# Five raw weight buffers for four, four low-word buffers for five, and one gather moved into the middle of an expert's second layer

## The chip, the cores and the metric

The kernel runs on one core of one Trainium2 chip. The metric is the device time of one execution in microseconds (us). The engines go by short names: PE is TensorE (PEld its weight loads), ACT ScalarE, DVE VectorE, POOL GpSimd, SP SyncE, whose queue issues the plain transfers; POOL issues the indirect ones (gathers and scatters of rows).

## The reference, cut to what matters

Three stages follow each other on 1792 rows of 768 numbers, all in float32: an attention with a sigmoid for a softmax, a layer of eight experts in which each expert takes 224 rows, and a wide layer of 2048.

```python
attn = 1.0 / (1.0 + np.exp(-scores))            # 4 x 12 heads of 448 x 448
x = np.matmul(attn, v)                          # 1792 x 768 after a transposition
...
for e in range(E):                              # E = 8, cap = 224 rows each
    mask = assigned == e
    h = np.maximum(x[mask] @ w1[e], 0.0)        # 768 -> 1024
    out[mask] = h @ w2[e]                       # 1024 -> 768
...
r = np.maximum(x @ w_in, 0.0)                   # 768 -> 2048
return (s * (r * r) + b) @ w_out                # 2048 -> 768
```

Which rows go to which expert is settled by a bidding of all rows for all experts.

## The kernel before, in words

**Two words for one number.** PE multiplies in a format that keeps fewer bits than float32. So each operand is split into a high word (the number in that format) and a low word (what is left), and each product is taken as high by high, high by low and low by high. For a weight tile this is a chain of three steps: SP asks for the raw tile of 128 x 768 float32 (384 KB) into the pool `wraw`; ACT casts it to the high word `wh` (line 242, `w_high`, pool `wsp` with five buffers); DVE, for some tiles POOL, subtracts to get the low word `wl` (line 252, `w_low`, pool `wlp`). The raw buffer is free again when the low word is done; the low-word buffer is free again when PE's last product with it is done.

**One list of tiles.** All weight tiles of the expert layer and of the wide layer stand in one list, `units`, in the order in which PE uses them. Counters say how far each step of the chain has come: `dma`, `pre`, `high`, `low`, and `use` for PE. After each step of PE's work `advance()` (line 752) moves them on: requests up to 8 tiles past `use`, low words up to `use + ahead - 1`, high words up to `use + ahead`, with `ahead` 5 (3 or 4 in the mixed layer). What an engine has in its queue is run in order, so a low word that stands behind a slow instruction waits with it.

**An expert** (`expert`, line 774; they are counted from 0 here, as in the code). Its first layer has eight steps, one weight tile each: six by `half_mm`, in which one matmul of 448 columns takes high and low word of the input side by side, and two by `short_mm`. Its second layer has six steps of eight pairs of matmuls; its eight tiles hold six column blocks each, so a step eats one tile and a third. After the matmuls of a step, ACT copies half of the sum out of PSUM (line 718), DVE adds the other half (719), `advance()` follows, and then `done` splits the result into high and low word for the next layer (lines 725 and 726, or 780 and 781).

**Rows of the experts.** `gather(e)` (line 603) has POOL fetch an expert's 224 rows by index in two parts of 128 and 96 rows, 3 KB each, into the two buffers of the pool `xrp`. `x_split(e, n)` turns a quarter of them on PE (704) and splits them on ACT and DVE (706, 707); for experts 6 and 7 this stands in the first layer of the expert before. So a gather must come after the last `x_split` of the expert before it and before the first of its own. For experts 6 and 7 it is issued between the two layers of experts 4 and 5. During the first layer of expert 4 POOL also issues six scatters of result rows (line 853).

**After the experts.** Experts 0 and 1, and 2 and 3, are followed by `layer_in` (the wide layer's first half for 448 rows); after 3 comes `outputs` (the second half), which writes 896 rows. After expert 7 come `layer_mixed` and `outputs` once more; there some tiles are sums and differences of others, formed on DVE in `w_pre`.

Of the kernel before, what the change touches and what calls it, by code (L numbers as in the profile page):

```python
# [28 lines left out]
KD = DM // 128  # L29
KF = F1 // 128  # L30
# [33 lines left out]
def tile_kernel(ctx, tc, qT, kT, v, wg, w1, w2, wi, wo, s2, b2, cst, out):  # L64
# [1 line left out]
    V, A, G, T = nc.vector, nc.scalar, nc.gpsimd, nc.tensor  # L66

    const = ctx.enter_context(tc.tile_pool(name="const", bufs=1))
    wraw = ctx.enter_context(tc.tile_pool(name="wraw", bufs=4))
    wsp = ctx.enter_context(tc.tile_pool(name="wsp", bufs=5))  # L70
    wlp = ctx.enter_context(tc.tile_pool(name="wlp", bufs=5))
    xrp = ctx.enter_context(tc.tile_pool(name="xrp", bufs=2))
    dpool = ctx.enter_context(tc.tile_pool(name="dpool", bufs=1, space=DRAM))
    ctx.enter_context(tc.manual_schedule())
# [103 lines left out]
    raws, splits, sums = {}, {}, {}  # L178
    nu = {"dma": 0, "pre": 0, "high": 0, "low": 0, "use": 0, "ahead": 5}
# [14 lines left out]
    for g in range(4):  # L194
# [3 lines left out]
        more = [narrow[f] for f in range(KG)] if g < 2 else []  # L198
        if g == 3:
            more = [(0, 1), (1, 1), (0, 2), (1, 2), (0, 3), (1, 3), (0, 4)]  # L200
# [45 lines left out]
    def w_low(eng=None):  # L246
        i = nu["low"]
        if i < nu["high"]:
            r, h = w_source(i), splits[i]
            lo = wlp.tile([128, KD, 128], F32R, name="wl")[:, :r.shape[1]]  # L250
            eng = eng or (G if where[i] else V)
            eng.tensor_sub(lo, r, h.bitcast(F32))  # L252
            splits[i] = (h, lo)
            nu["low"] += 1

    def w_get():
        i = nu["use"]
        nu["use"] += 1
        return splits.pop(i)
# [343 lines left out]
    def gather(e):  # L603
        if e >= E:
            return
        for h, n in enumerate(HT):
            if (e, h) not in xr:
                xr[e, h] = xrp.tile([128, DM], F32, name="xr")
            G.indirect_dma_start(out=xr[e, h][:n], out_offset=None, in_=xs,
                                 in_offset=bass.IndirectOffsetOnAxis(ap=idx[:n, h, e:e + 1], axis=0))  # L610
# [69 lines left out]
    def row_ids():  # L680
        def put(dst, rows, h, col, r0, n, src):
            for r in range(0, n, 32):
                G.tensor_copy(dst[rows + r:rows + r + 32, col], idx[r0 + r:r0 + r + 32, h, src])

        a, b = slice(0, E, 2), slice(1, E, 2)
        put(idt[:, 0], 0, 0, slice(0, 4), 64, 64, a)
        put(idt[:, 0], 64, 1, slice(0, 4), 0, 64, a)
        put(idt[:, 1], 0, 1, slice(0, 4), 64, 32, a)
        put(idt[:, 1], 32, 0, slice(0, 4), 0, 96, b)
        put(idt[:, 2], 0, 0, slice(0, 4), 96, 32, b)  # L690
        put(idt[:, 2], 32, 1, slice(0, 4), 0, 96, b)
        put(idl, 0, 0, slice(0, 2), 0, 64, slice(0, 4, 2))
        put(idl, 64, 0, slice(0, 2), 0, 64, slice(4, E, 2))
# [15 lines left out]
    def half_mm(weights, src, n, done, ahead, tt=None):  # L709
        p = ps_m.tile([128, 512], F32, name="acc")  # L710
        for k in range(n):
            wh, wl = weights(k)
            T.matmul(p[:, :2 * CAP], wh, src[:, k].rearrange("p a s -> p (a s)"), start=(k == 0), stop=False)  # L713
            T.matmul(p[:, :CAP], wl, src[:, k, 0], start=False, stop=(k == n - 1))  # L714
        t2 = pool["y"].tile([128, 2, CAP], F32, name="tmp", bufs=pool["tmp"])
        bs = t2[:, 0]
        tt = t2[:, 1] if tt is None else tt
        A.copy(bs, p[:, CAP:2 * CAP])  # L718
        V.tensor_add(tt, p[:, :CAP], bs)
        if ahead:  # L720
            advance()
        done(tt, bs)

    def two(dst, src):
# [13 lines left out]
    def w_dmas():  # L738
        while nu["dma"] < min(nu["use"] + 8, len(units)):
            w_dma()  # L740

    def w_lows():
        while nu["low"] < min(nu["use"] + nu["ahead"] - 1, nu["high"]):
            w_low()

    def w_highs():
        while nu["high"] < min(nu["use"] + nu["ahead"], len(units)):
            if nu["pre"] == nu["high"]:
                w_pre()
            w_high()  # L750

    def advance():
        w_dmas()
        w_lows()
        while nu["pre"] < min(nu["use"] + nu["ahead"] + 1, nu["dma"]):
            w_pre()
        w_highs()
# [16 lines left out]
    def expert(e, y):  # L774
        x = xg.pop(e)
        u = ml.tile([128, KF, 2, CAP], F32R, name="u")

        def first(f):
            def done(tt, _):
                A.activation(u[:, f, 0], tt, AF.Relu)  # L780
                V.scalar_tensor_tensor(u[:, f, 1], tt, 0.0, u[:, f, 0].bitcast(F32), op0=ALU.max, op1=ALU.subtract)  # L781

            return done

        for f in range(KF):
            wh, wl = w_get()
            if f < KF - 2:
                half_mm(lambda k: (wh[:, k], wl[:, k]), x, KD, first(f), f < KF - 3)
                if f == KF - 3:
                    advance()  # L790
            else:
                short_mm(wh, wl, x, KD, (u[:, f, 0], u[:, f, 1]))
                if f == KF - 2:
                    advance()
            if 1 <= f <= 4 and (e % 2 == 0 or e == 5):
                x_split(e + 1, f - 1)
            if f >= 1 and out_rows:
                scatter(*out_rows.pop(0))
        if e in (4, 5):
            gather(e + 2)  # L800
        sl = slice((e % 2) * CAP, (e % 2 + 1) * CAP)
        held = []
        if e == 6:
            mov["b22"] = m2p.tile([128, HK, 2, S], F32R, name="x")
        elif e == 7:
            mov["t3"] = m2p.tile([128, HK, 2, S], F32R, name="x")

        def halves(name, d, cols=sl):
            return mov[name][:, d, 0, cols], mov[name][:, d, 1, cols]

        for d in range(KD):
            def second(k):
                n, c = divmod(d * KF + k, KD)
                if n == len(held):
                    held.append(w_get())
                return [w[:, c] for w in held[n]]

            def done(tt, spare):
                if e < 6:
                    two((y[:, d, 0, sl], y[:, d, 1, sl]), tt)  # L820
                    return
                if d < HK:
                    V.tensor_sub(spare, tt, full(0, d, sl))
                    work = [(halves("t1", d), spare)]
                    if e == 7:
                        work.append((halves("t3", d, slice(0, CAP)), full(1, d, slice(0, CAP))))
                else:
                    V.tensor_sub(full(1, d - HK, sl), full(1, d - HK, sl), tt)
                    work = [(halves("b22", d - HK), tt)]
                    if e == 7:  # L830
                        work.append((halves("t3", d - HK), full(1, d - HK, sl)))
                for dst, src in work:
                    A.copy(dst[0], src)
                for dst, src in pending:
                    V.tensor_sub(dst[1], src, dst[0].bitcast(F32))
                pending[:] = work
                if e == 7 and d in (0, 1):
                    mix(2 - d, slice(0, CAP))

            tt = None  # L840
            if e in (4, 5):
                tt = full(d // HK * 2, d % HK, sl)
            elif e > 5 and d < HK:
                tt = full(1, d, sl)
            half_mm(second, u, KF, done, d < KD - 1, tt)
            if not e and d == 1:
                row_ids()
            if e == 1 and 2 <= d <= 4:
                late_do(f"a{d - 2}", 0)

    def scatter(ids, row):
        G.memset(spacer, 0.0)
        st = G.indirect_dma_start(out=out, out_offset=bass.IndirectOffsetOnAxis(ap=ids, axis=0), in_=row,
                                  in_offset=None)
        for o in stores:
            tc.declare_no_dep(st.ins, o.ins, reason="different rows")
        stores.append(st)
# [104 lines left out]
    def ahead(st, n, more=()):  # L962
        def lows():
            while na["low"] < min(n + 3, na["high"]):
                a_low(st)

        def sums():
            while na["sum"] < min(n + 5, 28):
                a_sum(st)

        w_dmas()
        work, more = [w_lows, lows, sums], list(more)
        while work or more:
            for q in (work, more):
                if q:
                    q.pop(0)()
        w_highs()
        while na["high"] < min(n + 4, 28):
            a_high(st)
# [261 lines left out]
```

## Time and profile before

| what | value |
|---|---|
| median of 3 runs | 916.81 us (915.82 to 917.8) |
| the profiled execution | 918.23 us, span 916.4 us |
| busy: PE, PEld | 879.4 us (96%), 755.4 us (82%) |
| busy: DVE, ACT, POOL | 659.4 us (72%), 519.5 us (57%), 130.0 us (14%) |
| mean transfer rate | 187 GB/s |

The span is the time from the first to the last instruction; the execution's own time has a little around it. A share of busy time is a mean over the whole kernel and says nothing of which engine holds up which in one stage. In a row of the timeline, the bracket at its end is the time that the engine was idle before the instruction, with what ended it. A raw tile is `raw`, its high word `wh`, its low word `wl`; `xr` are gathered rows, `px` and `acc` are tiles in PSUM.

### The profile page before, as it was taken

To read this page: it belongs to the slowest core of one execution; us is meant where nothing else is said; L and a number is where in the kernel's file an instruction comes from. 1 tells how busy PE (TensorE), PEld (TensorE's weight loads), DVE (VectorE), ACT (ScalarE), POOL (GpSimd) and SP (SyncE) were. 2 spreads that over 40 slices of the span, in tenths; PEclk is the share of its full clock that TensorE was granted. 3 is DMA by queue.
4 is the path that set the end of the run, shared out by engine and by line. 5 is a ranking of instruction groups with operands and counts; after the bars stand their busy time and mean duration, and the time that the engine had idled before them with its cause. 6 is when DMAs were issued, how large, how long until landed. Compare 5 with 4: busy or idle time off the path is not lost.

```text
span 916.4 us, 14216 instructions
## 1 busy us (share of the span) xinstructions
PE 879.4 (96%) x5219; PEld 755.4 (82%) x5219; DVE 659.4 (72%) x1101; ACT 519.5 (57%) x895; POOL 130.0 (14%) x131
## 2 busy tenths in 40 slices
PE   9999999789999999999999999899997999999997
PEld 4554555559989989999999998898996899999997
DVE  3877885646678777689767855877897788768680
ACT  6666666736555565643565545666655455654540
POOL 1000003222600033300000035422300000000003
PEclk9999999769999999999999999999998999999999
DMA  9989994755768775759643438665541212332213
GB/s 291 332 289 350 313 325 163 214 168 164 220 210 287 246 253 177 228 178 324 218 141 123 128 123 278 201 206 174 193 138 52 69 53 69 104 120 94 97 35 138
DMA packets 70186, 171.52 MB, mean 187 GB/s; under 512 B 8160, under 2 KB 25056, under 8 KB 70112
## 3 DMA queue, kind: packets, MB, share of 16 engines
q1 hardware_dynamic: 67840, 159.56, 53.3%
q0 software_dynamic: 2272, 11.01, 3.4%
q8 instruction: 42, 0.69, 0.3%
q14 instruction: 32, 0.26, 0.1%
HBM read 142.23 MB, written 28.31 MB: 186 GB/s over the span
## 4 chain that ended last, share of the span: by engine, by line
PE 52%; DVE 9%; DMA 7%; issue 5%; ACT 3%; POOL 1%; POOLq 0%; ACTq 0%; DVEq 0%; SPq 0%
DMA raw<-in_w_dram 7%; PE acc L1014 6%; PE acc L1016 6%; PE acc L1017 6%; PE acc L860 4%; PE acc L861 4%; PE acc L862 4%; PE acc L713 4%; DVE wl L252 4%; PE acc L1108 3%; PE acc L1106 3%; PE acc L1107 3%; PE acc L714 2%; ACT wh L242 1%; DVE u L781 1%
## 5 line engine op out<-in xcount | busy, mean ns | idle before, releaser
L242 ACT CAST wh<-raw 128x768 fp32r<-128x768 f32 (+1 forms) x240 | 195.5, 823 | 119.5 <-issue 48.0
L252 DVE TENSOR_TENSOR wl<-raw,wh 128x768 fp32r<-128x768 f32 (+1 forms) x199 | 191.9, 971 | 45.4 <-ACT wh L242 45.0
L252 POOL TENSOR_TENSOR wl<-raw,wh 128x768 fp32r<-128x768 f32 x41 | 82.5, 2016 | 439.9 <-ACT wh L242 439.8
L713 PE MATMUL acc<-u,wh 128*128 128x448 f32 x384 | 122.9, 378 | 1.6 <-DVE u L736 1.3
L714 PE MATMUL acc<-u,wl 128*128 128x224 f32 x384 | 102.3, 266 | 2.5 <-DVE wl L252 2.5
L302 ACT ACTIVATE attn<-psc,nls 112x896 f32<-112x896 f32 x96 | 88.8, 1008 | 10.1 <-PE psc L300 10.1
L713 PE MATMUL acc<-x,wh 128*128 128x448 f32 x288 | 93.7, 380 | 0.6 <-issue 0.6
L713 PEld LDWEIGHTS acc<-u,wh 128*128 128x128 f32 x384 | 72.8, 189 | 8.4 <-DVE u L736 3.0
L714 PE MATMUL acc<-x,wl 128*128 128x224 f32 x288 | 76.6, 266 | 2.3 <-DVE wl L252 2.3
L311 PE MATMUL pv<-attn,vt 112*64 112x448 f32 x384 | 77.5, 546 | 0.0
L714 PEld LDWEIGHTS acc<-u,wl 128*128 128x128 f32 x384 | 74.1, 193 | 2.8 <-DVE wl L252 2.8
L860 PE MATMUL acc<-y,wh 128*128 128x448 f32 x192 | 71.2, 371 | 0.9 <-ACT y L725 0.9
L861 PE MATMUL acc<-y,wh 128*128 128x448 f32 x192 | 70.6, 368 | 0.0
L862 PE MATMUL acc<-y,wl 128*128 128x448 f32 x192 | 70.3, 366 | 0.0
L311 PEld LDWEIGHTS pv<-attn,vt 112*64 112x64 f32 x384 | 25.4, 136 | 43.0 <-issue 36.1
L714 PEld LDWEIGHTS acc<-x,wl 128*128 128x128 f32 x288 | 55.0, 191 | 3.4 <-DVE wl L252 3.4
L713 PEld LDWEIGHTS acc<-x,wh 128*128 128x128 f32 x288 | 54.1, 188 | 4.5 <-issue 0.8
L1014 PE MATMUL acc<-wh,as 128*128 128x384 f32 x168 | 56.3, 335 | 0.0
L1017 PE MATMUL acc<-wh,as 128*128 128x384 f32 x168 | 56.2, 334 | 0.0
L1016 PE MATMUL acc<-wl,as 128*128 128x384 f32 x168 | 56.1, 334 | 0.0
L718 ACT COPY tmp<-acc 128x224 f32<-128x224 f32 x96 | 32.6, 340 | 21.1 <-PE acc L714 20.4
L781 DVE SCALAR_TENSOR_TENSOR u<-tmp,u 128x224 fp32r<-128x224 f32 x48 | 30.6, 639 | 18.0 <-ACT u L780 18.0
(341 smaller groups left out, 2027.9 us busy)
## 6 DMA issues: line engine op xcount, KB each, us to landing
raw<-in_w_dram SPq DMA_DIRECT2D x128, 384.0 KB, 3.5
raw<-nw SPq DMA_DIRECT2D x72, 384.0 KB, 3.2
craw<-in_wi_dram SPq DMA_DIRECT2D x16, 768.0 KB, 6.1
raw<-mx SPq DMA_DIRECT2D x32, 384.0 KB, 2.9
nw<-co SPq DMA_DIRECT2D x24, 384.0 KB, 6.9
craw<-in_wo_dram SPq DMA_DIRECT2D x8, 768.0 KB, 5.6
ra<-in_wo_dram SPq DMA_DIRECT2D x8, 768.0 KB, 6.4
rqk<-in_kT_dram SPq DMA_DIRECT2D x24, 224.0 KB, 6.6
```

Source lines behind the costliest of these rows:

```text
L242: A.copy(h, r)
L252: eng.tensor_sub(lo, r, h.bitcast(F32))
L302: A.activation(attn[n][:, :, c, :], p[:, :, :S], AF.Sigmoid, bias=nls[:CP], scale=1.0 / math.sqrt(D))
L311: T.matmul(pv[j * 64:(j + 1) * 64, :S], v[:, c, j * D:(j + 1) * D], a[:, j, c, :], start=(c == 0), stop=(c == NC - 1))
L713: T.matmul(p[:, :2 * CAP], wh, src[:, k].rearrange("p a s -> p (a s)"), start=(k == 0), stop=False)
L714: T.matmul(p[:, :CAP], wl, src[:, k, 0], start=False, stop=(k == n - 1))
L860: T.matmul(p, wh, src[:, k, 0], start=first, stop=False)
L861: T.matmul(p, wh, src[:, k, 1], start=False, stop=False)
L862: T.matmul(p, wl, src[:, k, 0], start=False, stop=last)
L1014: T.matmul(acc, hi, wh[:, cols], start=(opens[j] and u == 0 and c == 0), stop=False, skip_group_check=True)
L1016: T.matmul(acc, hi, wl[:, cols], start=False, stop=False, skip_group_check=True)
L1017: T.matmul(acc, lo, wh[:, cols], start=False, stop=(u == 3 and c == 1), skip_group_check=True)
```

## The change

The raw pool gets a fifth buffer and the low-word pool loses one; the memory is the same. `advance` takes a number: with 1, low words go as far ahead as before; with 2, one tile less far. The second layers of the experts and `outputs` use 2, first layers, `layer_in` and `layer_mixed` use 1. The gather of expert 6's rows moves from the end of expert 4's first layer to the third step of its second layer; that of expert 7's rows stays between the layers of expert 5.

```diff
-    wraw = ctx.enter_context(tc.tile_pool(name="wraw", bufs=4))
+    wraw = ctx.enter_context(tc.tile_pool(name="wraw", bufs=5))
     wsp = ctx.enter_context(tc.tile_pool(name="wsp", bufs=5))
-    wlp = ctx.enter_context(tc.tile_pool(name="wlp", bufs=5))
+    wlp = ctx.enter_context(tc.tile_pool(name="wlp", bufs=4))
...
         if ahead:
-            advance()
+            advance(ahead)
...
-    def w_lows():
-        while nu["low"] < min(nu["use"] + nu["ahead"] - 1, nu["high"]):
+    def w_lows(n=1):
+        while nu["low"] < min(nu["use"] + nu["ahead"] - n, nu["high"]):
             w_low()
...
-    def advance():
+    def advance(n=1):
         w_dmas()
-        w_lows()
+        w_lows(n)
...
-                half_mm(lambda k: (wh[:, k], wl[:, k]), x, KD, first(f), f < KF - 3)
+                half_mm(lambda k: (wh[:, k], wl[:, k]), x, KD, first(f), int(f < KF - 3))
...
-        if e in (4, 5):
-            gather(e + 2)
+        if e == 5:
+            gather(7)
...
-            half_mm(second, u, KF, done, d < KD - 1, tt)
+            half_mm(second, u, KF, done, 2 if d < KD - 1 else 0, tt)
             if not e and d == 1:
                 row_ids()
+            if e == 4 and d == 2:
+                gather(6)
...
-        work, more = [w_lows, lows, sums], list(more)
+        work, more = [lambda: w_lows(2), lows, sums], list(more)
```

The order in which the instructions stand, at three places. First SP's queue where expert 0's second layer begins: the transfer of a wide weight in raw form into `ra`, and then the first requests for raw tiles, with the semaphores that each waits for (DMAHW is a transfer's own, DVE, Pool and Activation the engines'). Before:

```order
L867 DMA ra_2744<-in_wo_dram 128x1536 [waits Activation_sequencer_49,PE_sequencer_49,Pool_sequencer_49,DVE_sequencer_49,DVE_49,SP_sequencer_49,PE_49,DMAHW4_49,Activation_49,Pool_49]
L218 DMA raw_2769<-in_w2_dram 128x768 [waits DMAHW5_49,DVE_49,Activation_49]
L218 DMA raw_2793<-in_w2_dram 128x768 [waits DMAHW6_49,Pool_49]
L218 DMA raw_2826<-in_w2_dram 128x768 [waits DMAHW7_49,DVE_49]
L218 DMA raw_2856<-in_w2_dram 128x768 [waits DMAHW0_49,DVE_49,Activation_49]
```

and now:

```order
L869 DMA ra_2744<-in_wo_dram 128x1536 [waits Activation_sequencer_49,PE_sequencer_49,Pool_sequencer_49,DVE_sequencer_49,DVE_49,SP_sequencer_49,PE_49,DMAHW4_49,Activation_49,Pool_49]
L218 DMA raw_2769<-in_w2_dram 128x768 [waits DMAHW5_49]
L218 DMA raw_2793<-in_w2_dram 128x768 [waits DMAHW6_49,DVE_49,Activation_49]
L218 DMA raw_2826<-in_w2_dram 128x768 [waits DMAHW7_49,DVE_49,Activation_49]
L218 DMA raw_2856<-in_w2_dram 128x768 [waits DMAHW0_49,Pool_49]
```

The requests are the same and stand in the same order, but the waits have moved down by one: the first request waits for no low word any more, and POOL's low word is waited for two requests later.

Second, POOL's queue from expert 4's first layer (the last two scatters into `out_dram`) to the gathers into `xr` for experts 6 and 7. Before:

```order
L853 DMA out_dram<-rb,idt 1792x768
L609 DMA xr<-xs,idx 128x768
L609 DMA xr<-xs,idx 96x768
L252 TENSOR_TENSOR wl<-raw,wh 128x768 x5
L609 DMA xr<-xs,idx 128x768
L609 DMA xr<-xs,idx 96x768
L252 TENSOR_TENSOR wl<-raw,wh 128x768 x11
```

and now:

```order
L855 DMA out_dram<-rb,idt 1792x768
L252 TENSOR_TENSOR wl<-raw,wh 128x768
L609 DMA xr<-xs,idx 128x768
L609 DMA xr<-xs,idx 96x768
L252 TENSOR_TENSOR wl<-raw,wh 128x768 x4
L609 DMA xr<-xs,idx 128x768
L609 DMA xr<-xs,idx 96x768
```

The first gather stands behind one low word, that of the fifth tile of expert 4's second layer, where it stood ahead of it. In the same way POOL's gathers after experts 0 and 2 now stand ahead of one low word that came before them.

Third, DVE from the fifth step of expert 7's second layer (line 719 is the addition that empties PSUM) into the mixed layer. Before:

```order
L719 TENSOR_TENSOR tmp<-acc,tmp 128x224
L252 TENSOR_TENSOR wl<-raw,wh 128x768
L252 TENSOR_TENSOR wl<-xr,wh 128x768
L231 TENSOR_TENSOR raw<-raw 128x384
...
L770 TENSOR_TENSOR rb<-rb,ra 128x3x224
L1077 TENSOR_TENSOR u<-ra,u 128x3x448
L1122 TENSOR_TENSOR tmp<-acc,tmp 128x448
L1123 SCALAR_TENSOR_TENSOR tmp<-tmp 128x448
L252 TENSOR_TENSOR wl<-xr,wh 128x768
```

and now:

```order
L719 TENSOR_TENSOR tmp<-acc,tmp 128x224
L252 TENSOR_TENSOR wl<-raw,wh 128x768
L231 TENSOR_TENSOR raw<-raw 128x384
...
L770 TENSOR_TENSOR rb<-rb,ra 128x3x224
L1079 TENSOR_TENSOR u<-ra,u 128x3x448
L252 TENSOR_TENSOR wl<-xr,wh 128x768
L1124 TENSOR_TENSOR tmp<-acc,tmp 128x448
L1125 SCALAR_TENSOR_TENSOR tmp<-tmp 128x448
L252 TENSOR_TENSOR wl<-xr,wh 128x768
```

The first low word that is made from `xr`, of the mixed layer's third tile, has moved from ahead of line 231 to behind the subtraction of line 1077 (1079 now).

## Rows read from the trace of the kernel before

**Rows 1.** The page's first part: busy time, share of the span, instructions.

```profile
PE 879.4 (96%) x5219; PEld 755.4 (82%) x5219; DVE 659.4 (72%) x1101; ACT 519.5 (57%) x895; POOL 130.0 (14%) x131
```

**Rows 2.** Windows: second layers of experts 1, 3, 4, 5 (columns in the first row).

```profile
core 0: us, PE busy (x) PEld busy (x) DVE busy (x) ACT busy (x) POOL busy (x), PEclk, DMA share, GB/s
253.44:269.75 16.31, 15.57 (x98) 14.36 (x97) 11.33 (x22) 11.36 (x22) 2.19 (x1) 1.00 0.69 217
380.09:396.41 16.32, 15.57 (x99) 14.36 (x97) 10.01 (x20) 10.67 (x22) 2.18 (x1) 1.00 0.71 226
560.85:580.05 19.20, 16.68 (x98) 15.62 (x97) 8.09 (x14) 8.64 (x18) 5.44 (x4) 0.91 0.71 234
599.41:614.44 15.03, 15.03 (x98) 14.35 (x97) 9.65 (x14) 9.07 (x18) 5.70 (x3) 1.00 0.66 208
```

**Rows 3.** Timeline of PE, five stalled matmuls: start, us, line, operation, idle before.

```profile
274.06 0.47 PE L860 MATMUL acc<-y,wh 128*128 128x448 f32 x1 [0.90 <-ACT y L725]
...
366.46 0.37 PE L714 MATMUL acc<-x,wl 128*128 128x224 f32 x1 [0.73 <-DVE wl L252]
...
573.14 0.55 PE L714 MATMUL acc<-u,wl 128*128 128x224 f32 x1 [2.52 <-DVE wl L252]
...
591.04 0.30 PE L704 MATMUL px<-ident,xr 96*128 96x96 f32 x1 [1.84 <-DVE x L707]
...
695.70 0.74 PE L1108 MATMUL acc<-x,wl 128*128 128x448 f32 x1 [5.22 <-DVE wl L252]
```

**Rows 4.** Waits of ACT: us in total, times, longest.

```profile
ACT wh L242 <- DMA raw<-in_w_dram: 33.8, 26, 3.6
```

**Rows 5.** Waits of SP's transfer queue, same columns.

```profile
SPq L218 <- DVE wl L252: 481.4, 178, 21.2
```

**Rows 6.** Timelines of DVE and SP in expert 2: low words and one request.

```profile
348.05 0.95 DVE L252 TENSOR_TENSOR wl<-raw,wh 128x768 fp32r<-128x768 f32 x1
...
351.89 0.95 DVE L252 TENSOR_TENSOR wl<-raw,wh 128x768 fp32r<-128x768 f32 x1
...
352.92 0.33 SPq L218 DMA_DIRECT2D raw<-in_w_dram  x1
```

**Rows 7.** Timeline of ACT: two high words that waited, experts 1 and 4.

```profile
246.17 0.83 ACT L242 CAST wh<-raw 128x768 fp32r<-128x768 f32 x1 [3.61 <-DMA raw<-in_w_dram]
...
570.39 0.83 ACT L242 CAST wh<-raw 128x768 fp32r<-128x768 f32 x1 [2.94 <-DMA raw<-in_w_dram]
```

**Rows 8.** Timeline of POOL in expert 4: first part of the gather, low word.

```profile
559.47 1.12 POOL L609 DMA_INDIRECT xr<-xs,idx  x1 [0.30 <-issue]
...
564.77 2.17 POOL L252 TENSOR_TENSOR wl<-raw,wh 128x768 fp32r<-128x768 f32 x1 [2.94 <-ACT wh L242]
```

**Rows 9.** Windows of 10 us around the gather, columns as in rows 2.

```profile
540.00:550.00 10.00, 10.00 (x65) 9.76 (x63) 3.05 (x6) 6.07 (x12) 4.81 (x5) 1.00 0.35 110
...
560.00:570.00 10.00, 10.00 (x69) 9.59 (x68) 2.54 (x5) 3.00 (x5) 3.69 (x3) 1.00 0.98 325
```

**Rows 10.** Transfers issued from 559 to 571: issues, us to landing.

```profile
xr<-xs,idx POOLq DMA_INDIRECT x2, 9.0
```

**Rows 11.** Window of the low clock in expert 4, columns as in rows 2.

```profile
572.70:576.11 3.41, 2.97 (x10) 2.80 (x11) 3.41 (x4) 1.03 (x3) 1.83 (x1) 0.50 0.55 174
```

**Rows 12.** Timelines of POOL and DVE in expert 5: low words side by side.

```profile
587.55 1.85 POOL L252 TENSOR_TENSOR wl<-raw,wh 128x768 fp32r<-128x768 f32 x1 [0.43 <-ACT wh L242]
...
587.59 2.62 DVE L252 TENSOR_TENSOR wl<-raw,wh 128x768 fp32r<-128x768 f32 x1
```

**Rows 13.** Timeline of DVE from expert 7 into the mixed layer.

```profile
684.14 0.95 DVE L252 TENSOR_TENSOR wl<-xr,wh 128x768 fp32r<-128x768 f32 x1
...
693.49 0.62 DVE L1122 TENSOR_TENSOR tmp<-acc,tmp 128x448 f32<-128x448 f32 x1 [1.81 <-ACT tmp L1113]
```

**Rows 14.** Timelines of SP and PE in expert 0.

```profile
208.71 0.33 PE L704 MATMUL px<-ident,xr 128*128 128x128 f32 x1 [0.17 <-DMA xr<-xs,idx]
...
210.45 0.34 SPq L218 DMA_DIRECT2D raw<-in_w_dram  x1
```

## The prediction, made before the changed kernel ran

> **What bounds the kernel now.** I read the page first: TensorE (PE) is busy for 96% of the span [rows 1]. A change that adds and removes no matmul can win only what PE loses in stalls, so the next view is the stalls one by one, then the views that tell why each happened.
>
> The second layer of an expert is six steps of eight matmul pairs. Without a stall it takes 15.03 us, as in expert 5: 2.51 us a step, 1.88 us a weight tile. Experts 1 and 3 take 16.31 and 16.32, expert 4 takes 19.20 [rows 2]: 1.28, 1.29 and 4.17 us lost. PE's own rows name what ended the longest waits [rows 3]: 0.73 us and 2.52 us for a low word in experts 3 and 4, 1.84 us for the low half of a transposed input (one of two such waits, in experts 5 and 6), 5.22 us for a low word where the mixed layer starts, 0.90 us for the last y where the layer after expert 1 starts.
>
> Why low words are late stands two engines further back. ScalarE (ACT) makes the high word of each tile and waited 33.8 us in 26 places for the raw tile to land [rows 4]. The transfer queue, in turn, sat 481.4 us waiting for VectorE's (DVE's) low words [rows 5]: a request leaves when the low word of an older tile frees a raw buffer. One example [rows 6]: the low word of 351.89 is finished at 352.84, the request leaves at 352.92. So with four raw buffers it is the buffer's round trip that sets the pace. ACT works in order, so while it waits for a tile, the copies that empty PSUM stand behind it; PE feels it some steps later.
>
> **The change, part by part.** No instruction is added or removed on any engine, and the order of the transfers is the same; three things move.
>
> *The fifth raw buffer.* Where the low words keep their place (first layers, the layer after experts 1 and 3, the mixed layer), a request needs the low word of one tile earlier. In the example it is the one that ended at 349.00 instead of 352.84 [rows 6]: 3.9 us earlier; elsewhere about one tile, 1.9 us. In experts 1 and 3 ACT waited 3.61 us for one tile (row of 246.17, one of two alike) [rows 7]; PE paid with the 1.28 and 1.29 us above and the 0.73 us. I expect most of those 3.3 us back, since 1.9 to 3.9 us of lead stand against waits of 3.6: **-2.6 us** (bounds 0 and -3.3). The gathers that follow experts 0 and 2 in POOL's queue run about 2 us earlier too, since one low word now stands behind them; they keep colliding with the same tiles, which is why I do not take all.
>
> *The gather of expert 6's rows.* It was issued at 559.47, right behind six scatters [rows 8], into the one stretch in which the DMA engines are full: share 0.98 and 325 GB/s from 560 to 570 us, after 0.35 from 540 to 550 [rows 9]; its two halves took 9.0 us to land [rows 10]. ACT then waited 2.94 us for a tile until 570.39 [rows 7], PE 2.52 us until 573.14, and, after that pause, PE had from 572.70 on 3.41 us of a granted clock of 0.50 (the lower level, 1.2 GHz) [rows 11], 2.97 us of it busy, which costs 1.5 us. Now the gather stands behind POOL's low word of 564.77 [rows 8], which ends at 566.94, after the scatters. It moves 224 rows of 3 KB, 0.69 MB, or 2.1 us of full engines, out of the tile's way, and the tile that the fifth buffer fetches ahead while the engines are at 0.35 takes away 0.39 MB or 1.2 us more. The late tile would come 3.3 us earlier: from ACT's start to PE's restart were 2.75 us, so PE could go on at about 569.9, and PE's wait began at 570.62 (573.14 less 2.52). The wait and the low clock go: **-3.6 us** of the 4.17 (bounds 0 and -4.2), since the margin is only 0.8 us. What is late next: the gather must land before PE transposes the rows, two steps into expert 5's first layer; that layer began at 580.05 [rows 2] and would now begin near 576, and from 567 even 9.0 us of landing would just do.
>
> *The transposes.* The two waits of about 1.85 us [rows 3] come from an evacuation that is behind, and it is behind for two reasons: ACT's waits for tiles, and a low word on DVE that took 2.62 us beside one on POOL of 1.85 us [rows 12], where 0.95 is usual [rows 6]. The first reason shrinks, the second stays. I take half: **-1.8 us** (bounds 0 and -3.7). The Trainium skill (SBUF — State Buffer, "Who interferes with whom") says that DVE and GpSimd share one pair of ports as an exclusive lock, so that the later of the two blocks to the end of the other. The DVE row agrees: it ended 0.8 us after POOL's. By that rule alone this term would be 0 and the forecast 909.5, inside its own range.
>
> *One low word later.* In second layers the low words run one tile less ahead, in four buffers for five. In expert 7's fifth step the low word of 684.14 leaves DVE's full chain and is made after line 1077's subtraction, where DVE sits idle for 1.81 us before 693.49 [rows 13]. The wait of 5.22 us for the next low word shortens by what left the chain: **-0.9 us** (bounds 0 and -0.9). In the same way one low word less stands ahead of the last y before 274.06: **-0.8 us** of 0.90 (bounds 0 and -0.9). What it may cost: in each second layer the low word of the seventh tile comes after the third step instead of the second. PE reads it one step and four pairs later (2.51 + 1.25, or 3.8 us); the copy, the addition and the low word of 0.95 us want under 2. It costs nothing while ACT is not held by a tile for more than about 2 us.
>
> *The start.* The first tile of expert 0's second layer left at 210.45, held by a low word [rows 14]; in the new order it waits for no low word, so it leaves with the transfer ahead of it in the queue, beside the gather of expert 1's rows, for which PE waited 0.17 us at 208.71. Its 0.39 MB is 1.2 us at 325 GB/s; if all of it came ahead of the gather, PE would wait that much more, if none, nothing. Half: **+0.6 us** (bounds 0 and +1.2). In the attention stage, where the low-word pool serves too, each of its writes comes well after the last read of the buffer it now takes: 0.
>
> Sum: -2.6 - 3.6 - 1.8 - 0.9 - 0.8 + 0.6 = -9.1 us. The profiled execution took 918.23, so 909.1 by it; it lies 1.4 above the median of 916.81, and against that the forecast is **907.7 us**. With all bounds on one side the sum is -13.0, on the other +1.2.
>
> **Rivals.** (1) *The engines, not the buffers.* If the tiles are late because the DMA engines are full, a fifth buffer makes requests stand longer in the queue and nothing else. For it: 0.98 in rows 9. Against it: that is one stretch of 10 us, and in the second layers of experts 1 and 3 the share is 0.69 and 0.71, hardly more than in expert 5, which has no stall (0.66) [rows 2]. Then only the gather's own 2.1 us, the two moved low words and the start remain: -2.1 - 1.7 + 0.6 = -3.2, 913.6 us. The Trainium skill (DMA: Bandwidth & Descriptors, "Issuing engines are not separate DMA queues") says that transfers of all issuing engines end on the same 16 DMA engines and interleave there, which is the rule behind this rival; rows 9 and 10 agree for that stretch.
>
> (2) *The gather meets expert 5's tiles.* At 567 the queue asks for the tiles of expert 5's first layer. If the gather costs them the 2.1 us that it no longer costs expert 4, and PE's clock falls again for about 1.5 us, 3.6 us come back: 911.3 us. Against it: the scatters have landed by then, and 2 us of lead have been won.
>
> (3) *Slower: too few low words ahead.* If ACT goes on being held by tiles for more than 2 us, the low word of the seventh tile comes after PE wants it, in each of the eight second layers, by up to its own 0.95 us: +7.6, less the 3.6 of the gather, 920.8 us. It decides only where the waits of rows 4 stay as long as 2.94 or 3.61 us; the requests that leave earlier speak against it.
>
> (4) *No effect.* PE's waits come from DVE beside POOL, and earlier tiles wait in SBUF: what the moved low words win, the start and a wait for four buffers take: 916.8 us. The wait of 2.94 us in rows 7 speaks against it.
>
> **How the numbers follow.** Forecast 0.62, rivals 0.13, 0.08, 0.08 and 0.09 in their order. About 0.2%, 1.8 us, is what a measurement of this kernel can tell from no change. Forecast and rivals 1 and 2 are faster by more: 0.83. Rival 4 is the same: 0.09. Rival 3 is slower: 0.08. The range goes from 902.5, all bounds on the good side and 1.3 us for stalls that I did not list, to 914.5, which takes in rivals 1 and 2; it leaves out rivals 3 and 4.
>
> **What would show it.** ACT's waits for raw tiles fall from 33.8 us to under 15; the second layers of experts 1, 3 and 4 come near 15.03 each; the low-clock stretch at 573 is gone; PE's waits for transposed inputs are about halved; the wait at the mixed layer's start is near 4.3 us; PE waits up to 1 us more near 209. I am wrong if ACT waits for tiles as long as before, if PE's waits for low words in second layers grow, or if expert 5 shows the stall that expert 4 lost.

## The result, and the profile after

The changed kernel takes 901.99 us (median of 4 runs, 901.41 to 903.45), the kernel before beside it 917.30 (4 runs, 915.82 to 918.67): a ratio of 0.9836, 95% interval 0.9816 to 0.9856. So it is 15 us faster, where 9 were forecast, and it lies just below the range. The profiled executions say the same: spans of 901.7 and 916.4 us, 14.7 us apart, for the same 5219 matmuls.

Since no matmul changed, PE's time splits at the same places in both traces. Windows of the changed kernel, in the order second layers of experts 1, 3, 4 and 6, then first layers of experts 1, 2, 3, 7, 5 and 6 (us, then each engine's busy time with its count, granted clock, DMA share, GB/s):

```profile
252.85:268.28 15.43, 15.29 (x98) 14.34 (x97) 12.77 (x23) 10.89 (x22) 2.19 (x1) 1.00 0.71 214
375.10:390.13 15.03, 15.03 (x98) 14.35 (x97) 9.74 (x17) 9.23 (x20) 2.20 (x1) 1.00 0.66 205
553.61:568.64 15.03, 15.03 (x98) 14.35 (x97) 7.22 (x12) 8.06 (x16) 6.21 (x5) 1.00 0.90 307
621.08:637.37 16.29, 15.30 (x98) 14.35 (x97) 12.03 (x19) 9.25 (x19) 5.91 (x3) 1.00 0.59 178
...
237.21:252.85 15.64, 15.57 (x111) 14.79 (x109) 13.10 (x20) 9.31 (x21) 6.65 (x4) 1.00 0.85 271
328.28:344.76 16.48, 16.48 (x121) 15.96 (x120) 12.52 (x24) 12.73 (x28) 4.80 (x3) 1.00 0.78 260
359.80:375.10 15.30, 15.30 (x110) 14.79 (x109) 12.61 (x21) 10.43 (x23) 6.11 (x4) 1.00 0.82 245
637.37:652.67 15.30, 15.30 (x110) 14.80 (x109) 13.85 (x24) 10.16 (x23) 4.49 (x3) 1.00 0.68 216
568.65:588.12 19.47, 16.97 (x123) 15.93 (x121) 17.54 (x29) 13.35 (x31) 8.30 (x5) 1.00 0.64 211
603.15:621.08 17.93, 16.71 (x122) 15.94 (x121) 15.83 (x27) 12.00 (x27) 4.24 (x3) 1.00 0.61 184
```

The first three answer to [rows 2]: 16.31, 16.32 and 19.20 have become 15.43, 15.03 and 15.03. First layers were not among the rows before; the same view of the kernel before has, for experts 1, 2, 3 and 7:

```profile
237.14:253.44 16.30, 16.00 (x110) 14.93 (x109) 12.65 (x21) 8.57 (x20) 6.89 (x5) 1.00 0.71 228
331.14:348.44 17.30, 16.97 (x121) 15.84 (x120) 13.44 (x24) 12.37 (x27) 4.12 (x3) 1.00 0.70 227
363.48:380.09 16.61, 15.83 (x111) 14.87 (x109) 13.41 (x21) 9.41 (x22) 7.65 (x5) 1.00 0.64 202
648.06:664.64 16.58, 15.57 (x111) 14.79 (x109) 13.80 (x25) 11.33 (x26) 6.00 (x3) 1.00 0.55 183
```

66.79 us in all became 62.72, at a higher DMA share: the engines had room. The stretch from the end of expert 7 to the end of PE's next long wait (for line 1113, now 1115), before and then after:

```profile
680.05:722.72 42.67, 35.30 (x164) 31.30 (x162) 35.53 (x61) 23.09 (x40) 0.00 (x0) 0.92 0.14 46
```

```profile
668.47:708.02 39.55, 33.54 (x165) 30.09 (x163) 34.81 (x60) 22.99 (x40) 0.00 (x0) 1.00 0.17 57
```

Sorted by stage, with the terms of the prediction's sum beside what the two traces give (the gather's -3.6 stands where it was to be won):

| stage | before | after | measured | forecast |
|---|---|---|---|---|
| second layers of experts 1, 3 and first layers of 1, 2, 3, 7 | 99.42 | 93.18 | -6.2 | -2.6 |
| second layer of expert 4 | 19.20 | 15.03 | -4.2 | -3.6 |
| first layers of experts 5, 6 | 37.94 | 37.40 | -0.5 | -1.8 |
| layers after experts 1, 3, with outputs | 209.35 | 207.00 | -2.4 | -0.8 |
| second layers of experts 6, 7 | 30.44 | 32.09 | +1.7 | 0 |
| mixed layer's start | 42.67 | 39.55 | -3.1 | -0.9 |
| all up to the end of expert 0 | 237.14 | 237.21 | +0.1 | +0.6 |

The rows add up to -14.7, the whole difference; the stages that are not in the table agree within 0.1. Each column is one execution, and a single stage can differ by 1 us with no edit near it: run e1 below is the kernel before up to expert 4, and expert 3's second layer, 16.32 us before, takes 15.61 in it, its first layer 15.48 instead of 16.61.

```profile
379.45:395.06 15.61, 15.30 (x98) 14.36 (x97) 9.32 (x17) 9.20 (x18) 2.19 (x1) 1.00 0.70 226
```

So a row of the table says where time went, and the medians say how much.

What is left of PE's waits, in its timeline after (start, us, idle before and releaser), answers to [rows 3] and [rows 14]:

```profile
209.38 0.33 PE L704 MATMUL px<-ident,xr 128*128 128x128 f32 x1 [1.22 <-DMA xr<-xs,idx]
...
571.87 0.37 PE L714 MATMUL acc<-x,wl 128*128 128x224 f32 x1 [0.96 <-DVE wl L252]
...
579.73 0.30 PE L704 MATMUL px<-ident,xr 96*128 96x96 f32 x1 [1.53 <-DVE x L707]
...
612.70 0.30 PE L704 MATMUL px<-ident,xr 96*128 96x96 f32 x1 [1.22 <-DVE x L707]
...
635.60 0.37 PE L714 MATMUL acc<-u,wl 128*128 128x224 f32 x1 [0.99 <-DVE wl L252]
...
679.39 0.47 PE L1110 MATMUL acc<-x,wl 128*128 128x448 f32 x1 [3.05 <-DVE wl L252]
...
682.49 0.47 PE L1110 MATMUL acc<-x,wl 128*128 128x448 f32 x1 [1.01 <-DVE wl L252]
```

And ACT's waits for raw tiles [rows 4] have fallen from 33.8 us to 9.9 (total, times, longest):

```profile
ACT wh L242 <- DMA raw<-in_w_dram: 9.9, 7, 2.9
```

### The profile page after: what moved, and what is told of

The parts are those of the page before. It is cut to its first block, busy times and chain, and to the rows that moved or that the text cites. A ratio compares the mean times of both kernels' runs of the same rounds, so it can differ in the third digit from the quotient of the medians.

```text
span 901.7 us, 14232 instructions
## 1 busy us (share of the span) xinstructions
PE 872.2 (97%) x5219; PEld 753.2 (84%) x5219; DVE 658.0 (73%) x1101; ACT 520.6 (58%) x895; POOL 129.2 (14%) x131
## 4 chain that ended last, share of the span: by engine, by line
PE 64%; DVE 7%; DMA 3%; issue 2%; ACT 2%; POOL 0%; POOLq 0%; ACTq 0%; DVEq 0%; SPq 0%
PE acc L713 10%; PE acc L1018 6%; PE acc L1016 6%; PE acc L1019 6%; PE acc L714 5%; PE acc L862 4%; PE acc L864 4%; PE acc L863 4%; PE acc L1110 3%; PE acc L1108 3%; PE acc L1109 3%; DVE wl L252 2%; DMA raw<-in_w_dram 2%; PE acc L731 1%; PE acc L733 1%
## 5 line engine op out<-in xcount | busy, mean ns | idle before, releaser
L252 DVE TENSOR_TENSOR wl<-raw,wh 128x768 fp32r<-128x768 f32 (+1 forms) x199 | 194.8, 983 | 14.1 <-PE acc L1018 10.1
L719 DVE TENSOR_TENSOR tmp<-acc,tmp 128x224 f32<-128x224 f32 x78 | 30.0, 384 | 25.9 <-ACT tmp L718 25.5
```

## The experiments

Twelve runs, each beside the kernel before on the same chip; kernels that ran together shared it. My theory at first was that of the prediction: fifth buffer, gather and low words each win their own time.

**The three parts apart (e1, e2, e3).** In e2 and e3 all else is as in the change. e1 is the kernel before with the gather alone moved, and its lines are shown against that kernel.

```diff
# e1: four raw, five low-word buffers, low words as before
-        if e in (4, 5):
-            gather(e + 2)
+        if e == 5:
+            gather(7)
...
+            if e == 4 and d == 2:
+                gather(6)
# e2: the change, without that edit
# e3: e2, with
-    wraw = ctx.enter_context(tc.tile_pool(name="wraw", bufs=5))
+    wraw = ctx.enter_context(tc.tile_pool(name="wraw", bufs=4))
```

> The kernel before, with only the gather of expert 6's rows moved into expert 4's second layer (four raw and five low-word buffers, as before). Theory (the three parts act each for itself): the gather is worth what the second layer of expert 4 loses, 4.17 us, less what a tile that is fetched no earlier still loses (up to 1.2 us), so that layer falls from 19.20 to between 15.0 and 16.3 us and the time by 2.9 to 4.2 us, to 913.1 to 914.4; ACT's waits for raw tiles fall by some 3 us only, to about 31. Rival (the gather only meets other tiles): the second layer of expert 4 gets short, the first layer of expert 5 longer by as much, and the time stays at 917.

> The changed kernel with the gather of expert 6's rows put back ahead of expert 4's second layer; buffers and low words as in the change. Theory (separate parts): the second layer of expert 4 is back at 18 to 19.2 us with its low clock, all else is as in the changed kernel, so 3.0 to 4.2 us more than its 902.0: 905.0 to 906.2. Rival (the fifth raw buffer alone carries PE over the gather): the second layer of expert 4 stays under 16 us and the time under 903.5.

> Four raw buffers, four low-word buffers, the low words one tile less ahead in second layers and outputs, the gather at its old place: the one part of the change that should cost something, alone. Theory (the raw buffer's round trip sets the pace): a later low word frees its raw buffer later, so ACT's waits for raw tiles rise above 33.8 us, second layers get longer, and the 2 to 3 us that the layer after expert 1 and the mixed layer's start win are taken back: 916 to 922. Rival (the DMA engines set the pace, the buffers don't): ACT's waits stay at 33 to 35 us and the gains of the moved low words are left over, 914 to 915.

On one chip, the kernel before at 915.78 (23 runs): e1 took 915.21, ratio 1.0001 (0.9981 to 1.0022); e2 900.65, ratio 0.9836 (0.9816 to 0.9857), the change's own ratio to the last digit; e3 919.96, ratio 1.0054 (1.0031 to 1.0078). So the gather's move is worth nothing that these runs can tell, alone or on top: alone, the interval leaves room for at most 0.2%, and the forecast 2.9 to 4.2 us lie outside it. The low words that run less ahead, with one buffer fewer, cost 0.5% alone, and **the fifth raw buffer, the one difference between e3 and e2, is worth 19.3 us beside these low words**. What it is worth with low words as before was not run; both parts together, without the gather, win 15.1 us (915.78 to 900.65). The rival of e2 holds, and of e1 neither text holds whole: its profile has (second layer of expert 4, first layers of 5 and 6)

```profile
560.27:575.30 15.03, 15.03 (x98) 14.35 (x97) 7.85 (x13) 7.91 (x16) 6.84 (x4) 1.00 0.83 285
575.31:595.48 20.17, 16.99 (x123) 15.94 (x121) 17.56 (x29) 14.13 (x32) 8.44 (x5) 1.00 0.63 209
610.51:630.53 20.02, 18.30 (x123) 17.39 (x121) 16.62 (x29) 12.27 (x28) 4.33 (x3) 0.91 0.52 160
```

The 4.17 us in expert 4 are won as priced, but the next two first layers are 0.81 and 1.44 us longer (19.36 and 18.58 before), the second of them with a granted clock of 0.91 for 1.00. That gives back 2.25 of the 4.17; the medians show no gain, and where the rest goes is not shown. In e2 the gather stands where it stood before:

```profile
551.59 1.49 SPq L218 DMA_DIRECT2D raw<-in_w_dram  x2
```

```profile
552.67 0.99 POOL L609 DMA_INDIRECT xr<-xs,idx  x1 [0.30 <-issue]
```

```profile
552.80:568.59 15.79, 15.30 (x98) 14.37 (x97) 9.68 (x13) 9.18 (x18) 8.03 (x5) 1.00 0.85 280
568.60:586.47 17.87, 16.71 (x123) 15.95 (x121) 16.07 (x29) 12.19 (x28) 6.50 (x4) 1.00 0.75 233
```

The gather's halves take 8.0 us to land here, hardly less than the 9.0 of [rows 10]. But the seventh tile's request (the first of the two in SP's row) now leaves ahead of them and needs 6.1 us to land; before it left at 560.96, behind the gather of 559.47 [rows 8], and needed 9.3. That is what ended the 2.52 us of [rows 3]: expert 4's second layer costs 0.76 us too much instead of 4.17. The change, with the gather moved, saves those 0.76 and pays them back in expert 5's first layer, 19.47 us against 17.87 here: there stands the 0.96 us wait of 571.87, which e2 does not have. That is the prediction's second rival, in small.

ACT's waits for raw tiles in e1, e2 and e3, each from its own profile, order the three runs:

```profile
ACT wh L242 <- DMA raw<-in_w_dram: 30.7, 33, 3.0
```

```profile
ACT wh L242 <- DMA raw<-in_w_dram: 8.5, 6, 2.9
```

```profile
ACT wh L242 <- DMA raw<-in_w_dram: 41.0, 39, 2.8
```

With four buffers a later low word frees its buffer later and ACT waits longer: the theory of e3, against its rival that the engines set the pace. Two of e3's rows sort the parts further. PE still waits for the last y after expert 1 as before, and the first layer of expert 7 takes 15.30 us as in the change, where the kernel before took 16.58 (and e8, below, 16.59):

```profile
273.34 0.47 PE L860 MATMUL acc<-y,wh 128*128 128x448 f32 x1 [0.90 <-ACT y L725]
```

```profile
651.18:666.48 15.30, 15.30 (x111) 14.80 (x109) 12.69 (x23) 10.30 (x24) 4.83 (x3) 1.00 0.69 212
```

So for the first the fifth buffer is needed and the moved low words do not do it; the second, 1.28 us, is the low words' gain and needs no fifth buffer. The wait that expert 7 loses is this one of the kernel before:

```profile
651.32 0.37 PE L714 MATMUL acc<-x,wl 128*128 128x224 f32 x1 [1.00 <-DVE wl L252]
```

**Low words at the mixed layer's start (e4, e5).** Both add two low words ahead of `mix(1, half)`; e5 also moves ACT's copy of `t4`, the fourth operand, from ahead of the first evacuation into a list of work done between later products.

```diff
+        w_low()
+        w_low()
         mix(1, half)
...
# e5 only
-        A.copy(mov["t4"][:, :, 0], srcs["t4"])
-        rest = [lambda: V.tensor_sub(mov["t4"][:, :, 1], ...)]
+        rest = [lambda: V.tensor_sub(mov["t4"][:, :, 1], ...),
+                lambda: A.copy(mov["t4"][:, :, 0], srcs["t4"])]
```

> The changed kernel, with two low words moved in DVE's order at the start of the mixed layer: they are made ahead of the addition and the subtraction for the next operand, not behind them. Theory (PE waits there for low words that stand at the end of DVE's chain): the waits of 3.05 and 1.01 us fall to some 0.8 us together, 3.2 us less: 898.8. Rival (the chain itself is the limit: what moves up pushes the operand back, and PE waits as long for it two products later): 901.5 to 902.5.

> The changed kernel with the two low words of run e4 ahead in DVE's order, and ACT's copy of the fourth operand's high words (1.31 us) taken off ACT's way: it is issued at the third pair of products instead of ahead of the first evacuation. Theory (in run e4 the waits for low words fell from 4.06 to 0.74 us, and what PE lost in their place, 1.37, 1.17 and 1.18 us, was ACT standing at that copy until DVE's subtraction was done): those three go too, and PE waits some 1 us in all here instead of 4.06: 902.0 less 3.0, or 899.0. Rival (the additions and subtractions of the start are the limit in any order): PE waits 3 to 4 us in other places, 901.5 to 904.

e4 took 904.31, ratio 0.9874 (0.9851 to 0.9898), slower than e2 on the same chip by 3.7 us. e5 took 904.78, 0.9876 (0.9837 to 0.9914). PE's timeline in e4:

```profile
676.60 0.47 PE L1112 MATMUL acc<-x,wl 128*128 128x448 f32 x1 [0.74 <-DVE wl L252]
...
681.49 0.47 PE L1110 MATMUL acc<-u,wh 128*128 128x448 f32 x1 [1.37 <-ACT tmp L1117]
...
684.75 0.47 PE L1110 MATMUL acc<-u,wh 128*128 128x448 f32 x1 [1.17 <-ACT tmp L1117]
...
688.02 0.47 PE L1110 MATMUL acc<-ra,wh 128*128 128x448 f32 x1 [1.18 <-ACT tmp L1117]
```

The wait for low words fell as forecast, from 4.06 to 0.74 us, and came back as three waits for ACT, which copies only after DVE's subtraction. With that copy out of the way (e5) it came back once more:

```profile
673.54 0.47 PE L1112 MATMUL acc<-x,wl 128*128 128x448 f32 x1 [0.72 <-DVE wl L252]
...
684.26 0.47 PE L1110 MATMUL acc<-ra,wh 128*128 128x448 f32 x1 [2.38 <-ACT tmp L1117]
```

In e5 a third wait, 0.92 us at 679.78, also ends with ACT. Both rivals hold in kind, and both times lie above their ranges: what one wait lost, others took. That the work of DVE and ACT as a whole is the limit at this place fits the two orders tried; no run with less of that work shows it.

**DVE beside POOL (e6).** In the first layers of experts 5 and 6, DVE makes the low words that POOL made.

```diff
-            where += [n in ((0, 2, 4, 6, 12) if e else (6, 12)) for n in range(2 * KF)]
+            where += [n in (((12,) if e in (5, 6) else (0, 2, 4, 6, 12)) if e else (6, 12)) for n in range(2 * KF)]
```

> The changed kernel, in which the four low words of the first layer that GpSimd makes for expert 5, and the four for expert 6, are made by VectorE. Theory (a low word on DVE that took 2.31 us beside one on POOL of 1.86, and a 1.52 us operation beside one of 2.18, are what keeps the evacuation of the transposes late): the two waits for transposed inputs, 1.53 and 1.22 us, and the one of 0.96 us at the start of expert 5 fall to under 1 us together: 2.7 us less, 899.3. Rival (DVE has no time for four more low words of 0.95 us in a first layer, in which it is 9 tenths busy): the waits grow, 904 or more. Rival two (the waits come from ACT and the tiles): no change, 902.

e6 took 898.94, ratio 0.9815 (0.9778 to 0.9851), with all six runs from 897.64 to 900.02. Run e7 on the same chip, which is as long as the change (below), had all of its six from 901.02 to 902.99, so e6 is some 3 us shorter: the theory. First layers of experts 5 and 6:

```profile
568.63:585.12 16.49, 16.49 (x122) 15.98 (x121) 15.59 (x32) 13.16 (x29) 2.17 (x2) 1.00 0.75 248
600.16:616.65 16.49, 16.49 (x123) 15.98 (x121) 14.31 (x28) 12.26 (x27) 0.00 (x0) 1.00 0.62 207
```

19.47 and 17.93 us became 16.49 each with PE busy throughout, and DVE, with three more low words in each of these windows, was busy for 15.59 and 14.31 us instead of 17.54 and 15.83. Over the whole kernel it made eight more (1109 instructions for 1101) and was busy for 654.5 us instead of 658.0:

```profile
PE 870.5 (97%) x5219; PEld 753.6 (84%) x5219; DVE 654.5 (73%) x1109; ACT 521.3 (58%) x895; POOL 113.9 (13%) x123
```

In the change the row that held the transposes is this pair, as in [rows 12]:

```profile
576.24 1.86 POOL L252 TENSOR_TENSOR wl<-raw,wh 128x768 fp32r<-128x768 f32 x1
```

```profile
576.60 2.31 DVE L252 TENSOR_TENSOR wl<-raw,wh 128x768 fp32r<-128x768 f32 x1
```

A low word on POOL cost DVE more here than making it itself: with eight of 0.95 us added and 3.5 us less in all, each of the eight had cost it some 1.4 us. The Trainium skill (SBUF — State Buffer, "Who interferes with whom") states the exclusive lock on the port pair that DVE and GpSimd share; this run agrees, by 1.95 and 1.52 us less of DVE's busy time in the two windows.

**The start (e7).** One more tile is requested in the routing stage.

```diff
-AHEAD = (2, 3, 4, 5)
+AHEAD = (2, 3, 4, 5, 6)
```

> The changed kernel with the first tile of expert 0's second layer requested during the routing stage (at about 185 us, where a fifth raw buffer is free), not at 202.32 just ahead of the gather of expert 1's rows. Theory (that tile shares the engines with the gather, whose first half took 5.9 us to land against 4.7 before): the gather lands within 4.7 us again, PE's wait at 209.38 falls from 1.22 to about 0.2 us and the time by 1.0, to 901.0. Rival (the other transfer that leaves beside it, 768 KB into the buffer of the next weights, is what slows the gather): the wait stays at 1.2 us and the time at 902.

901.94, ratio 0.9847 (0.9811 to 0.9884): no difference from the change. The wait fell only to 0.88 us:

```profile
208.28 0.33 PE L704 MATMUL px<-ident,xr 128*128 128x128 f32 x1 [0.88 <-DMA xr<-xs,idx]
```

That is 0.34 us less than in the change's profile, but the change's other profile (e12) has 0.68 without the edit:

```profile
208.33 0.44 PE L704 MATMUL px<-ident,xr 128*128 128x128 f32 x2 [0.68 <-DMA xr<-xs,idx]
```

So e7 shows nothing of the tile's share in that wait; its rival, the transfer of 768 KB, was not tried.

**The eighth tile (e8), and versions that go further (e9 to e12).**

```diff
# e8
-            half_mm(second, u, KF, done, 2 if d < KD - 1 else 0, tt)
+            half_mm(second, u, KF, done, (2, 2, 1, 2, 2, 0)[d], tt)
# e9: e6 and e8 together
# e10: e8, with
-            where += [n in ((0, 2, 4, 6, 12) if e else (6, 12)) for n in range(2 * KF)]
+            where += [n in ((12,) if e else (6, 12)) for n in range(2 * KF)]
# e11: e2 with that one line; e12: the change unaltered
```

> The changed kernel, but after the third step of each second layer the low words run as far ahead as before the change (the eighth tile is made there; its buffer is free by then). Theory (the waits of 0.99 us in expert 6's last step and of 0.36 us in expert 7's, which the kernel before does not have, are the price of low words that run one tile less ahead: the low word of the eighth tile starts 1.0 us before PE wants it): both go, 1.3 to 1.7 us less than 902.0, or 900.3 to 900.7. Rival (those waits come from DVE beside POOL, whatever the order): they stay, 902.

> Runs e6 and e8 in one kernel: the eight low words of experts 5 and 6 on VectorE, and the eighth tile's low word after the third step. Theory (each takes away waits that the other leaves): 898.9 less 1.3 to 1.7, so 897.2 to 897.6. Rival (with the four low words of expert 6 off POOL the wait in its second layer is gone or moves by itself, so the two overlap): 898.5 to 899.

> As e9, with the four low words of the first layer that POOL makes for experts 1, 2, 3, 4 and 7 on VectorE too. Theory (DVE beside POOL costs time only where a wait stands in the profile, and in these five experts the changed kernel has next to none): no more gain, 897 to 898. Rival (POOL costs DVE time everywhere, and the time so won shortens other stages): under 896. Rival two (DVE gets too full where it has transposes beside the y of the layer ahead): over 899.

> Run e10 without its two smaller edits: the first layers' low words on VectorE, the gather of expert 6's rows back at its old place, and the eighth tile's low word where the changed kernel has it. Theory (with five raw buffers the gather's place is worth nothing, and the eighth tile's earlier low word only moves waits): as run e10, 896 to 898. Rival (e10's lead over e9 hangs on the two): 899 to 901.

> The changed kernel once more, beside e11 on the same chip: 902, or 0.982 to 0.986 of the kernel before. The run says by how much e11 beats it. If e11 is the better one through the low words on VectorE, this one is 4 to 6 us longer than e11; if what the profiles of e6, e9 and e10 show is lost again elsewhere, under 2 us.

e8 took 903.15, ratio 0.9854 (0.983 to 0.9877), no gain. Second layer of expert 6 and first layer of expert 7 in it:

```profile
619.11:634.13 15.02, 15.02 (x98) 14.34 (x97) 10.87 (x17) 7.22 (x15) 4.33 (x2) 1.00 0.55 170
634.14:650.73 16.59, 15.57 (x111) 14.79 (x109) 14.27 (x25) 11.53 (x28) 5.94 (x3) 1.00 0.64 214
```

The wait of the eighth tile went as the theory said (16.29 to 15.02), and expert 7's first layer gave it back (15.30 to 16.59): PE waits 1.02 us for a low word there, as the kernel before did at 651.32. e9 took 898.54, 0.9792 (0.9772 to 0.9813): as e6, its rival. e10 took **896.89**, 0.9769 (0.9747 to 0.979), just under its theory's 897 and not told apart from e9 on that chip (894.66 to 900.85 against 896.56 to 898.97). e11 took 897.46, 0.9799 (0.9762 to 0.9835), and the change beside it 902.48, 0.986 (0.9819 to 0.9901): 5.0 us apart, with no run of the one among the other's (896.47 to 898.47, 900.73 to 904.11). So the first layers' low words are better made on VectorE in this kernel, and neither the gather's new place nor e8's edit is needed for it. For experts 5 and 6 e6 shows it alone; what the other five experts add is not told apart in the times, and in e11's profile expert 3's first layer takes 16.45 us, from 359.31 to 375.76, where the change takes 15.30.

The profile of e11 also shows what e8 left open. Second layer of expert 6 and first layer of expert 7 in it:

```profile
617.33:632.35 15.02, 15.02 (x98) 14.34 (x97) 10.85 (x20) 9.14 (x19) 2.14 (x1) 1.00 0.56 175
632.36:647.66 15.30, 15.30 (x110) 14.80 (x109) 14.09 (x28) 11.12 (x24) 0.00 (x0) 1.00 0.74 244
```

Neither the 0.99 us of the one nor e8's 1.02 us of the other is there, though the eighth tile's low word stands where the change has it (e2, which differs from e11 by POOL's low words alone, takes 16.27 us for the first of the two). In the change this pair of DVE and POOL came just ahead of that low word:

```profile
631.56 2.04 DVE L823 TENSOR_TENSOR tmp<-ra 128x224 f32<-128x224 f32 x1
```

```profile
631.21 2.14 POOL L252 TENSOR_TENSOR wl<-raw,wh 128x768 fp32r<-128x768 f32 x1 [4.02 <-ACT wh L242]
```

In e11, with expert 7's low words off POOL, the same subtraction of line 823 took 0.39 us. In e6, which leaves them on POOL, it took 2.05 and the wait of 0.99 us stayed. So e8's rival (DVE beside POOL) has the cause of that wait, and e8's edit moved it.

## Why the prediction was wrong, and where it was right

*What bounds the kernel* was right: the raw buffer's round trip. e3 against e2 shows it by one buffer alone, and the first rival (the DMA engines set the pace) falls with it. The fourth (no effect) falls with the result, but its mechanism, DVE beside POOL, is real: e6 and e11 win another 3 to 5 us by taking low words off POOL.

*The step that failed* is the fifth buffer's term, **-2.6 us with a bound of -3.3**. It was built from the stalls of two second layers and one wait in a first layer. These came as forecast (-2.17 and -0.73; the lead read from [rows 6] is 3.84 us and not 3.9, which changes nothing). The mechanism was right and the size too small, for the lead that a buffer gives is given to every tile. The first layers of experts 1, 2, 3 and 7 won another 3.3 us beside the 0.73, of which the 1.3 of expert 7 belong to the low words (e3); the layers after experts 1 and 3 and their outputs won 2.4 where 0.8 was counted, for another reason; and of expert 4's 4.17, 3.4 came without the gather's move (e2). The range allowed 1.3 us for all that was not listed. What the buffer measured alone, in medians and beside the later low words, is 19.3 us (e3 to e2).

*The gather's term*, -3.6, had the right size (4.17) by luck, for it had the wrong owner. "The gather ... out of the tile's way" was to win 2.1 us and the tile fetched ahead 1.2; e2 shows that the earlier request does 3.4 us of it without the move, and e1 that the move without the buffer is given back in experts 5 and 6 at least by half. The two terms were priced as a sum, though they were two cures for the same wait.

*The transposes*, -1.8: the two waits fell from 3.71 us to 2.75, by 1.0, not by half; a new wait of 0.96 us in expert 5's first layer stands against 0.54 before it. "The first reason shrinks, the second stays" was right, but the second is the larger: e6, which changes only who makes the low words, has none of the three waits.

*One low word later*, -0.9 and -0.8: the low word's wait of 5.22 us is 4.06 in two parts, so 1.2, and e3, with four raw buffers, has 3.54 and 0.64 there, so that reason was right. The wait for the last y is gone, but not for the reason given: e3 has the low words in their new place and still waits the 0.90 us. The mixed start won 3.1 because the granted clock there was 1.00 instead of 0.92 as well. I had costed such a clock at 573 and not at 692, where it stands in the same trace. It is no sure gain: the change's other profile (e12) has 0.96 over that start, and e2 has 0.92 there too,

```profile
666.71:707.80 41.09, 36.07 (x165) 32.54 (x163) 34.82 (x60) 23.10 (x40) 0.00 (x0) 0.92 0.16 55
```

and still wins 1.6 us at that place. *"It costs nothing while ACT is not held"* was wrong: second layers of experts 6 and 7 lost 1.7 us to low words, of which 1.3 came back in expert 7's first layer. The seventh tile was the one worked out; the eighth is tighter, and DVE, not ACT, holds it up: in expert 6 its high word starts at 628.00, its low word at 634.60, behind the 2.04 us beside POOL, and PE has waited 0.99 us for it by 635.60. That is what the third rival feared, a low word too late in a second layer, with another cause and at a fifth of its price (7.6).

*The start*, +0.6: PE's wait did grow by 1.05 us, near the bound of 1.2; the next wait there, 0.38 us for a transposed input, went, and the stage as a whole grew by 0.1. That the tile is the reason is not shown (e7).

Of the signs named, ACT's waits (under 15: 9.9), the second layers of experts 3 and 4, the clock at 573 and the wait at the mixed start (near 4.3: 4.06) came; the halved waits for transposes did not. PE's waits for low words in second layers, whose growth was named as a sign against, fell in all, from the 2.52 us in expert 4 to 0.99 and 0.36 in experts 6 and 7, which had none before.

What stays open is the wait at the start, and why e4 and e5 lose elsewhere as much as they win or more: their profiles show where the waits are, not what would end them.

## What to carry to other kernels

A buffer that closes a loop (request, landing, two conversions, release) can help every turn of that loop: price it over all stages in which that queue waits, small stalls too, not over the few longest stalls. Where two edits could both cure one wait, price each alone and both together before adding them. An engine that takes work off another only helps if the two do not slow each other where they overlap: add up the busy time of the one that was to be relieved, with and without.

## What was not expected of the hardware

DVE was busy for less time with more low words to make than with POOL making them: 14.31 us instead of 15.83 in expert 6's first layer, 15.59 instead of 17.54 in expert 5's. And a single raw buffer of 384 KB, four to five, moved the whole kernel by 19.3 us of 920 where low words run one tile less ahead, while the same transfers, engines and matmuls ran.
